# Cutting a sixth product of the second feed-forward stage into a two-level scheme, with two squarings moved to ScalarE

## The chip, the cores and the metric

The kernel runs on one core of a Trainium2 chip. The metric is the device time of one execution in microseconds (us).

## The reference, cut to what matters

An attention block without softmax feeds a feed-forward block whose activation is a scaled square of a relu. All arithmetic is fp32.

```
kv  = einsum('bhsd,bhse->bhde', k, v)            # 8 batches, 8 heads, 576 x 64
out = einsum('bhsd,bhde->bhse', q, kv)
x   = normalised out, transposed and reshaped to (4608, 512)
h   = x @ w_in                                   # 512 x 2048
g   = s * relu(h)**2 + b
y   = g @ w_out                                  # 2048 x 512
```

## The kernel before

The tokens are worked off in nine units of 512. A unit has a first stage (`x @ w_in`) and a second stage (`g @ w_out`). Each stage is a Strassen-Winograd scheme: 2 x 2 blocks, seven products (numbered 1 to 7) instead of eight, and additions on VectorE. From unit 2 on, five of the seven products of the second stage (`TWICE`) are cut up once more in the same way. The weight sums for this second level are formed once in unit 1 and written to DRAM.

```python
TWICE = (1, 2, 6, 7, 4)
ORDER = (1, 2, 6, 7, 5, 3, 4)      # the parts of a two-level product

def parts_of_w(i):                 # unit 1: four sums, seven stores of 256 KB
    ...
    for n, t in enumerate((y11, y21, t2, t3, t1, y22, t4)):
        nc.sync.dma_start(out=w3_dram[i][:, n], in_=t)

def second_level(i, other, to, x_tag="y", y_tag="y"):
    ...
    def go(m, bank, first):        # one part: 4 matmuls of 128x128 into one PSUM bank
        ...
        for f in range(FC // 4):
            matmul(t[bank], a[m][:, f], w[:, f], first and f == 0, f == FC // 4 - 1)
    def keep(name, j, q):          # VectorE reads the bank "x"
        scaled(r[name], t["x"], other(j, cols[q]))
    def m1(): go(1, "x", True);  keep("r1", 0, 0)
    def m2(): go(2, "z", True);  scaled(to(0, cols[0]), t["z"], r["r1"])
    def m6(): go(6, "x", False); keep("r2", 1, 0)
    def m7(): go(7, "y", True)
    def m5(): go(5, "x", False); keep("r4", 1, 1); scaled(to(1, cols[1]), t["y"], r["r4"])
    def m3(): go(3, "x", False); scaled(to(0, cols[1]), t["x"], other(0, cols[1]))
    def m4(): go(4, "y", False); scaled(to(1, cols[0]), t["y"], r["r2"])
```

Parts 1, 6, 5 and 3 add up in one bank "x" (a bank is a piece of PSUM, the memory into which the matmuls add their products), and VectorE reads the bank after each. So part 6 has to wait for the read after part 1, part 5 for that after part 6, part 3 for that after part 5. Something else must stand between them on PE. The scheduling is by hand: each engine gets its instructions in the order of the program. This is the end of a second stage, in program order:

```python
            p7[2]()                # p7[m]: part m of product 7
            pump(1)                # pump: load the next weight tiles into a ring of 7
            p7[6]()
            p7[7]()
            pump(1)
            p7[5]()
            at(3)                  # unit 2 only: an attention product
            def between():
                p7["sums"]((3,)); p4["sums"](); at("sums")
                p7[3](); pump(1); p7[4](); pump(1)
                at(("q", 0)); p4[1](); at("norm")
            x3(0, between)         # product 3, one level, row block 0: 8 matmuls of 128x256
            p4[2](); p4[6](); with_7(0); p4[7](); with_7(1)
            p4[5]()
            at(4)
            at(5)                  # the four sums xs for the next unit's first stage
            x3(1)                  # product 3, row block 1
            pump(4)
            at(("q", 1))
            y4_of(0, 3)            # part 3 of product 4, and stores
            pump(1)
            y4_of(1, 4)
```

## Time and profile before

| | |
|---|---|
| time, median of the first 3 runs | 953.24 us (953.16 to 955.73) |
| time, median of 6 runs, with those taken beside the changed kernel | 954.85 us |
| span of the profiled run | 951.5 us |
| PE busy | 936.3 us |
| one unit's end of second stage, from part 1 of product 6 to the next unit (units 3 to 7) | 25.66 us |

"PE" is the matmul row of TensorE and "PEld" its weight loads. "DVE" is VectorE, "ACT" is ScalarE and "SPq" is the sync engine's queue, which issues the DMAs. In a timeline each line has start, duration, engine, source line, operation, tiles, shape and count, with idle time and its releaser in brackets. All times of TensorE in this text are taken from start to start.

### The profile page before, as it was taken

The page shows a single profiled execution, that of the slowest core. Times are in us where ns is not written, and L with a number is a line of the kernel's source. Part 1 is how long each engine was busy: PE and PEld are TensorE (multiplying, and loading weights), DVE is VectorE, ACT ScalarE, POOL GpSimd, SP SyncE. Part 2 cuts the span into 40 slices and gives each one's busy share as a digit, 9 for nine tenths or more (in the row PEclk, how much of TensorE's full clock was granted, in tenths as well). Part 3 has the DMA queues.
Part 4 walks back from the last instruction along what each step waited for, and adds up shares of the span by engine and source line. Part 5 has one row for each costly group of instructions (what it writes and reads, how often), then busy time and mean ns, then how long its engine had stood idle before and what let it go on. Part 6 is the DMA issues. An engine that isn't in the chain of part 4 may idle for free.

```text
span 951.5 us, 17795 instructions
## 1 busy us (share of the span) xinstructions
PE 936.3 (98%) x7270; PEld 840.1 (88%) x7270; DVE 639.9 (67%) x1167; ACT 191.6 (20%) x366; POOL 6.7 (1%) x18
## 2 busy tenths in 40 slices
PE   7999999999999999999999999999999999999997
PEld 7888888888888998899889988999889988998997
DVE  2789667486567765876478656775678657854684
ACT  2784132101121013200231013101320032001100
POOL 2000000000000000000000000000000000000000
PEclk9999999999999999999999999999999999999999
DMA  9688726578772758165644764375526520653064
GB/s 248 199 317 247 251 79 195 138 221 258 192 190 55 234 155 225 24 193 190 178 110 130 236 185 111 85 248 162 158 51 220 185 92 12 209 180 121 14 222 142
DMA packets 136656, 158.46 MB, mean 167 GB/s; under 512 B 77696, under 2 KB 91776, under 8 KB 136448
## 3 DMA queue, kind: packets, MB, share of 16 engines
q1 hardware_dynamic: 133472, 155.57, 54.7%
q10 hardware_dynamic: 2784, 1.77, 0.8%
q8 instruction: 57, 0.93, 0.4%
q14 instruction: 23, 0.19, 0.1%
q0 software_dynamic: 320, 0.00, 0.0%
HBM read 131.34 MB, written 25.95 MB: 165 GB/s over the span
## 4 chain that ended last, share of the span: by engine, by line
PE 88%; DVE 5%; DMA 3%; ACT 2%; issue 1%; SPq 0%; DVEq 0%; ACTq 0%
PE x_ps L91 41%; PE y_ps L91 25%; PE z_ps L91 9%; PE t_ps L91 8%; PE x_ps L440 3%; PE kv_ps L377 2%; DMA w_raw<-in_moe_w_in_dram 1%; ACT xT L494 1%; DMA kv_sb<-in_k_dram 1%; DMA w_sb<-w 1%; DVE xT L488 1%; DVE a L247 1%; DVE xn L463 1%; DVE a L547 1%; DVE sub L250 0%
## 5 line engine op out<-in xcount | busy, mean ns | idle before, releaser
L592 ACT COPY r<-x_ps 128x512 f32<-128x512 f32 x96 | 56.0, 584 | 405.6 <-PE x_ps L91 383.3
L91 PE MATMUL x_ps<-xs,ws 128*128 128x256 f32 x512 | 122.1, 381 | 0.8 <-ACT r L592 0.4
L91 PE MATMUL y_ps<-xs,wb 128*128 128x256 f32 x512 | 122.6, 382 | 0.3 <-DVE a L247 0.3
L91 PEld LDWEIGHTS x_ps<-xs,ws 128*128 128x128 f32 x512 | 96.4, 190 | 15.9 <-ACT r L592 2.9
L91 PEld LDWEIGHTS y_ps<-xs,wb 128*128 128x128 f32 x512 | 95.5, 190 | 16.0 <-DVE a L247 2.5
L247 DVE TENSOR_TENSOR a<-y_ps,r 128x512 f32<-128x512 f32 x64 | 43.9, 685 | 72.1 <-ACT r L592 60.1
L91 PE MATMUL x_ps<-xT,wa 128*128 128x256 f32 x384 | 89.8, 380 | 0.1
L91 PEld LDWEIGHTS x_ps<-xT,wa 128*128 128x128 f32 x384 | 72.2, 190 | 10.5 <-ACT xT L494 0.5
L91 PE MATMUL x_ps<-w_sb,a 128*128 128x256 f32 (+1 forms) x376 | 79.7, 364 | 0.0
L91 PEld LDWEIGHTS x_ps<-w_sb,a 128*128 128x128 f32 x376 | 66.9, 190 | 8.4 <-issue 0.6
L547 DVE SCALAR_TENSOR_TENSOR a<-a 128x512 f32<-128x512 f32 x96 | 66.4, 691 | 3.1
L91 PE MATMUL y_ps<-w_sb,sub 128*128 128x128 f32 x504 | 62.0, 275 | 0.0
L91 PEld LDWEIGHTS y_ps<-w_sb,sub 128*128 128x128 f32 x504 | 60.2, 192 | 0.7
L91 PE MATMUL x_ps<-xT,ws 128*128 128x256 f32 x256 | 60.5, 379 | 0.0
L91 PE MATMUL z_ps<-xT,wa 128*128 128x256 f32 x256 | 60.5, 379 | 0.0
L91 PE MATMUL x_ps<-w_sb,s 128*128 128x256 f32 x256 | 58.1, 380 | 0.7 <-DMA w_sb<-w 0.7
L91 PE MATMUL t_ps<-w_sb,sub 128*128 128x128 f32 x448 | 54.8, 275 | 0.0
L91 PEld LDWEIGHTS z_ps<-xT,wa 128*128 128x128 f32 x256 | 48.6, 190 | 6.6
L626 DVE TENSOR_TENSOR a<-a 128x512 f32<-128x512 f32 x32 | 22.1, 689 | 47.9 <-ACT a L623 47.9
L91 PEld LDWEIGHTS x_ps<-w_sb,s 128*128 128x128 f32 x256 | 47.4, 190 | 7.2 <-issue 1.1
L91 PE MATMUL y_ps<-w_sb,a 128*128 128x128 f32 (+1 forms) x360 | 53.7, 298 | 0.0
L91 PEld LDWEIGHTS x_ps<-xT,ws 128*128 128x128 f32 x256 | 48.1, 190 | 6.2
(139 smaller groups left out, 1265.9 us busy)
## 6 DMA issues: line engine op xcount, KB each, us to landing
w_sb<-w SPq DMA_DIRECT2D x147, 512.0 KB, 4.9
w_sb<-w SPq DMA_DIRECT2D x35, 256.0 KB, 2.8
w_raw<-in_moe_w_in_dram SPq DMA_DIRECT2D x8, 1024.0 KB, 7.3
w_raw<-in_moe_w_out_dram SPq DMA_DIRECT2D x8, 1024.0 KB, 5.0
w_sb<-in_k_dram SPq DMA_DIRECT2D x48, 144.0 KB, 2.9
w_sb<-in_v_dram SPq DMA_DIRECT2D x48, 144.0 KB, 3.0
out_dram<-o SPq DMA_DIRECT2D x104, 64.0 KB, 2.6
w<-sub SPq DMA_DIRECT2D x20, 256.0 KB, 4.6
```

The lines of the kernel that those rows point to most:

```text
L91: nc.tensor.matmul(o, lhsT=lhsT, rhs=rhs, start=start, stop=stop, skip_group_check=True)
L247: nc.vector.tensor_tensor(out=o, in0=a, in1=b, op=ALU.add)
L377: nc.tensor.matmul(ps[r][l * HB : l * HB + HB, i, :], lhsT=kv[l][rows, 0, j, :], rhs=kv[l][rows, 1, j, :], start=(j == 0), stop=(j == R - 1),)
L440: nc.tensor.matmul(ps[32 * p : 32 * p + 32, w, :], lhsT=st["qT"][:, p, 32 * w : 32 * w + 32], rhs=bd_kv[(b if w < 2 else b1) % 2][:, p, :] ...
L463: nc.vector.tensor_tensor(out=st["xn"].rearrange("p h d -> p (h d)").rearrange("p (c h e) -> p h c e", c=KC, h=H), in0=st["x"].rearrange(" ...
L488: nc.vector.transpose(out=to, in_=st["xn"].rearrange("p h d -> p (h d)").rearrange("p (c x) -> p c x", c=KC))
L494: nc.scalar.activation(to[:, i], to[:, i], AF.Copy, scale=g_col[:, i : i + 1])
L547: nc.vector.scalar_tensor_tensor(t, t, 0.0, t, ALU.max, ALU.mult)
L592: nc.scalar.copy(st[name], src)
L626: nc.vector.tensor_mul(ga["a21", s], ga["a21", s], ga["a21", s])
```

## The change

Product 3 becomes the sixth two-level product. It has 28 matmuls of 128x128 instead of 16 of 128x256. As it no longer adds into product 5's bank, two adds (`with_5`) take over that sum. To make room on VectorE, two squarings of each unit's last step go to ScalarE. And the end of the second stage gets a new order, since the two halves of product 3 no longer exist.

```diff
-    TWICE = (1, 2, 6, 7, 4)
+    TWICE = (1, 2, 6, 7, 4, 3)
 ...
-            relu_sq(t)
+            if u > 1 and s == NS - 1:
+                nc.scalar.activation(t, t, AF.Relu)
+                nc.scalar.square(t, t)
+            else:
+                relu_sq(t)
 ...                                   # x3_square likewise, and it now follows x3 at once
-                lambda: x3(0),
+                seq(lambda: x3(0), lambda: parts_of_w(3)),      # unit 1
 ...
+        def with_5(j):
+            add(right("o1", j), right("o1", j), right("o2", j))
 ...
+            p7["sums"]((3,))
             p7[2](); pump(1); p7[6]()
+            p3["sums"]((5, 6))
             p7[7](); pump(1); p7[5](); at(3)
-            x3(0, between)
+            p3["sums"]((7, 3)); at("sums")
+            p7[3](); pump(1); p7[4](); pump(1)
+            with_5(0); at(("q", 0))
+            p3[1](); p4["sums"]((5, 6)); at("norm")
+            p3[2](); with_5(1); pump(1)
+            p3[6](); p4["sums"]((7, 3)); p3[7](); pump(1)
+            p3[5](); at(4)
+            p4[1]()
+            p3[3](); store("o1", 0, 4 * u); pump(1)
+            p3[4](); store("o1", 1, 4 * u + 1); pump(1)
+            at(5)
             p4[2](); p4[6](); with_7(0); p4[7](); with_7(1); p4[5]()
-            at(4); at(5); x3(1); pump(4)
+            pump(2)
             at(("q", 1)); y4_of(0, 3); pump(1); y4_of(1, 4); pump(1)
```

(Statements of several lines are put on one here.)

More of the change, by code (lines that the diff above doesn't have):

```diff
@@ L625, in x3_square @@
         def x3_square():
-            nc.vector.tensor_mul(ga["a21", s], ga["a21", s], ga["a21", s])
+            if u > 1 and s == NS - 1:
+                nc.scalar.square(ga["a21", s], ga["a21", s])
+            else:
+                nc.vector.tensor_mul(ga["a21", s], ga["a21", s], ga["a21", s])
         def x3_s1():
@@ L874, in x5, with x3 @@
                 store("o2", j, 4 * u + 2 + j, slice(HN, DM))
-        def x3(j, *between):
+        def x3(j):
             product(3, j, st["x", j], False)
-            for fn in between:
-                fn()
-            if u > 1:
-                add(right("o1", j), right("o1", j), b_21)
             scaled(rows("o1", j)[:, HN:], st["x", j], b2 if u == 1 else st["o1", j][:, HN:])
@@ L956, in mm2 @@
         )
+        p3 = second_level(3, lambda j, q: right("o1", j, q), lambda j, q: right("o1", j, q), "x")
         def x5_of(j, *between):
@@ L988, in rest @@
             step["x3"]()
+            step["x3_square"]()
             p2["sums"]()
@@ L991, in rest @@
             pump(1)
-            step["x3_square"]()
             p1[4]()
@@ L1038, in rest @@
             at(3)
-            def between():
-                p7["sums"]((3,))
-                p4["sums"]()
-                at("sums")
-                p7[3]()
-                pump(1)
-                p7[4]()
-                pump(1)
-                at(("q", 0))
-                p4[1]()
-                at("norm")
-            x3(0, between)
+            p3["sums"]((7, 3))
+            at("sums")
+            p7[3]()
+            pump(1)
+            p7[4]()
+            pump(1)
+            with_5(0)
+            at(("q", 0))
+            p3[1]()
+            p4["sums"]((5, 6))
+            at("norm")
+            p3[2]()
+            with_5(1)
+            pump(1)
+            p3[6]()
+            p4["sums"]((7, 3))
+            p3[7]()
+            pump(1)
+            p3[5]()
+            at(4)
+            p4[1]()
+            p3[3]()
+            store("o1", 0, 4 * u)
+            pump(1)
+            p3[4]()
+            store("o1", 1, 4 * u + 1)
+            pump(1)
+            at(5)
             p4[2]()
@@ L1058, in rest @@
             p4[5]()
-            at(4)
-            at(5)
-            x3(1)
-            pump(4)
+            pump(2)
             at(("q", 1))
```

## The prediction

> **What bounds the kernel now.** I read the page first. The busy table says that TensorE is the engine to watch, and the groups say how few and short its waits are.
>
> ```profile
> PE 936.3 (98%) x7270; PEld 840.1 (88%) x7270; DVE 639.9 (67%) x1167; ACT 191.6 (20%) x366; POOL 6.7 (1%) x18
> PEclk9999999999999999999999999999999999999999
> PE 88%; DVE 5%; DMA 3%; ACT 2%; issue 1%; SPq 0%; DVEq 0%; ACTq 0%
> ```
>
> PE is busy for 98% of the span at full clock, and the chain that ended last is PE for 88%. A PE gain should therefore reach the end, and so will any stall put into PE's stream. So I went to PE's timeline in one steady unit (the second stage of one unit in the middle, from 597 to 654 us). Columns: start, duration, engine, line, operation, shape, number of records. One fp32 matmul leaves two records, so a first-level product of one row block (8 matmuls of 128x256) is x16, and one of the seven parts of a second-level product (4 matmuls of 128x128) is x8.
>
> ```profile
> 635.85 2.84 PE L91 MATMUL y_ps<-w_sb,sub 128*128 128x128 f32 x24
> 638.53 3.62 PE L91 MATMUL x_ps<-w_sb,a 128*128 128x256 f32 x16
> 641.98 1.05 PE L91 MATMUL y_ps<-w_sb,sub 128*128 128x128 f32 x8
> 642.88 1.06 PE L91 MATMUL y_ps<-w_sb,a 128*128 128x128 f32 x8
> 643.77 1.06 PE L91 MATMUL t_ps<-w_sb,a 128*128 128x128 f32 x8
> 644.66 1.06 PE L91 MATMUL z_ps<-w_sb,a 128*128 128x128 f32 x8
> 645.55 2.84 PE L91 MATMUL t_ps<-w_sb,sub 128*128 128x128 f32 x24
> 648.24 3.62 PE L91 MATMUL x_ps<-w_sb,a 128*128 128x256 f32 x16
> 651.69 1.05 PE L91 MATMUL t_ps<-w_sb,sub 128*128 128x128 f32 x8
> 652.58 1.06 PE L91 MATMUL t_ps<-w_sb,a 128*128 128x128 f32 x8
> ```
>
> Start to start, the x16 takes 3.45 us and every x8 takes 0.893 us. There is no gap at all from 605 to 653.5 us: the dense second stage is pure PE throughput. The two x16 are product 3, the one that the change cuts up. They do a second job: each stands between part 5 of a two-level product and its part 3, which adds into the same PSUM bank. VectorE has 3.45 us to read the bank before PE needs it. VectorE's timeline there:
>
> ```profile
> 638.73 0.35 DVE L707 SCALAR_TENSOR_TENSOR r<-y_ps,s_col,o 128x128 f32<-128x128 f32 x1 [1.44 <-PE y_ps L91]
> 639.12 0.35 DVE L707 SCALAR_TENSOR_TENSOR or<-y_ps,s_col,r 128x128 f32<-128x128 f32 x1
> 649.09 0.68 DVE L250 TENSOR_TENSOR xs<-xT 128x512 f32<-128x512 f32 x1
> 651.62 0.42 DVE L247 TENSOR_TENSOR o<-o,b 128x256 f32<-128x256 f32 x1
> ```
>
> The first line is the read of part 5 (product 7), 1.1 us after that group's start; the last two bracket the four sums for the next unit, 2.53 us, wholly under the second x16.
>
> **What the Trainium skill says.** "PSUM — Partial Sum Buffer", section "Engine vs sequencer instructions": VectorE and ScalarE queues are strict FIFO, and matmuls start and complete in program order. So a matmul that waits holds all later ones, and a PSUM read behind long sums on VectorE waits for them. The trace agrees: both timelines keep the program's order. "VectorE: DVE Perf Modes", section "The TRN2 errata", gives (N+151)/0.96 ns for an fp32 tensor_tensor, 691 ns at 512 columns; the trace has 0.68 to 0.69 us, but successive ones start 0.60 us apart when independent and 0.72 apart when the second reads the first; I use those spacings. "Perfetto Trace Analysis", section "Tensor Engine Instruction", says that a matmul's end is estimated; so I take PE times from starts.
>
> **The change, part by part.** It concerns units 2 to 8, seven of them; unit 1 prepares the weights.
>
> *PE work.* Removed per unit: 2 x 3.45 = 6.91 us. Added: 7 parts x 0.893 = 6.25 us. Gain 0.66 us per unit, 4.6 us in all, 0.5%. This is all that the change can win, as PE has no wait there to lose.
>
> *VectorE to ScalarE.* Two squarings of about 0.6 us each leave VectorE in each unit's last step. ScalarE is 20% busy, and its copy of 128x512 takes 0.58 us. PE does not wait for VectorE there, so I give it nothing.
>
> *VectorE added.* Four sums of 128x512 (2.5 us), seven reads of 128x128 and two adds of 128x256, less four operations of 128x256: some 3.5 us more per unit, before the squarings. VectorE stays below 85% in these stages; its order matters, not its total.
>
> *New waits on PE.* The order listing shows that in the changed kernel product 7's part 5 is followed at once by its part 3, and likewise product 4's part 5 by part 3, each with a wait on VectorE. What such a wait costs: the read starts 1.09 us after the group's start (part 1 at 643.77, read at 644.86) and takes 0.35. The restart overhead comes from unit 2 of the kernel before, where VectorE was 0.08 us late for such a bank:
>
> ```profile
> 341.92 0.34 DVE L707 SCALAR_TENSOR_TENSOR r<-t_ps,s_col,or 128x128 f32<-128x128 f32 x1
> 342.32 0.97 PEld L91 LDWEIGHTS t_ps<-w_sb,sub 128*128 128x128 f32 x8 [0.15 <-DVE r L707]
> 340.40 3.07 PE L91 MATMUL t_ps<-w_sb,sub 128*128 128x128 f32 x24
> ```
>
> Three groups took 3.07 instead of 2.84, a loss of 0.23, so 0.15 beyond the lateness. A direct chain costs 1.09 + 0.35 - 0.893 + 0.15 = **0.70 us**.
>
> Now one unit by hand, with the first part of product 6 at 627.81 as origin, each group 0.893 later, and the order as listed:
> - Part 5 to part 3 of product 7: +0.70.
> - Part 1 of product 3 then starts at 641.01, is read at 642.10 to 642.37; two dependent sums for product 4 (1.33) end at 643.70; the next read (0.27) and an add (0.38) bring VectorE to 644.35, when it reads part 6; done 644.70. Part 5 wants that bank at 644.58: 0.12 + 0.15 = +0.27.
> - Part 4 of product 3 starts at 647.53 and is read at 648.62. Then VectorE does the four sums for the next unit (2.53), now ahead of product 4's parts 2 and 6 in its queue, and has read part 6 by 652.04. Part 5 of product 4 wants the bank at 651.11: 0.93 + 0.15 = +1.08. Before, these sums lay under the second x16.
> - Part 5 to part 3 of product 4: +0.70.
>
> Sum 2.75, less 0.66: **+2.1 us per unit**, for units 3 to 7: +10.5. Unit 8 makes no sums for a next unit: 0.70 + 0.27 + 0.70 - 0.66 = +1.0. Unit 2 has attention products between product 7's parts 5 and 3 (no first wait) but a row sum, a normalization and a transpose more in VectorE's queue; the same walk gives 1.10, 1.25 and 0.70, less 0.66: +2.4. Together +13.9 us.
>
> *Unit 1.* Four more subtractions (2.5 us) and seven more stores of 256 KB. VectorE is busy 13.8 of 25 us from 225 to 250 us, and PE is fed from tiles loaded long before: nothing.
>
> *Transfers.* A two-level product loads 1.83 MB instead of 1.05. Products 6, 7, 3 and 4 then take 7.3 MB in about 27 us, 272 GB/s; the queue moved 256 to 287 GB/s in the busiest 5 us stretches here, with up to seven tiles ahead. I worked out 3 to 4 us of lead for each tile: hidden.
>
> **The rivals.** (1) *PE work decides*: the waits are covered, the kernel gains 4.6 us, 948.6. For it: PE is gapless and the change is written to thin out VectorE. Against it: a wait straight after the matmul that it depends on cannot be covered by any VectorE. (2) *Mine*: the filler was worth more than the work saved, 967. (3) *Weights come late*: each of the seven units waits a further 1 to 2 us for a tile in products 3 and 4, 972 to 980. For it: demand is close to what the queue has shown, and the kernel before has one DMA wait of 0.7 us. Against: that one is the only one in seven units. (4) *ScalarE's squares or VectorE's relief* remove waits in the units' first parts: at most the 0.3 to 1 us per unit that PE idles in first stages, but those waits stand before the moved operations.
>
> **Range and chances.** 953.2 + 13.9 = **967.1**. The third wait is the least certain, as one VectorE operation earlier or later moves it by 0.5 us per unit, 3.5 in all; if the sums are covered in part, 962. More DMA waiting gives 971. Range 961.5 to 971. Slower by over 2% needs 972.3: 0.06. Faster by over 2% exceeds all that PE work can give: 0.01. Within 2%: 0.93.
>
> **What would show it right or wrong.** PE's timeline after product 7's part 5 and product 4's part 5 should show an idle of 0.4 to 0.5 us in the record (0.7 lost start to start), released by VectorE, in each of units 3 to 8; the one before product 4's part 5 should be absent in unit 8 and about 1.1 in units 3 to 7; x8 groups should keep 0.893. PE's sum of idle should grow by about 15 us and the waits of weight loads on VectorE likewise. If those gaps are missing and the end comes near 948.6, the read is quicker or the order different from what I took. If the gaps name DMA, rival 3 holds. If second stages look the same and first stages differ, rival 4.

## The result, and the profile after

The changed kernel took **971.5 us** (median of 6, 970.51 to 973.76) against 954.85 us for the kernel before. The ratio of fast runs is 1.0181 (95% interval 1.0164 to 1.0198). The profiled run has a span of 968.4 us, 16.9 more.

The page of the changed kernel: the busy shares, then the shares of the chain that ended last.

```profile
PE 938.0 (97%) x7438; PEld 842.9 (87%) x7438; DVE 659.6 (68%) x1220; ACT 204.8 (21%) x387; POOL 6.7 (1%) x18
PE 81%; DVE 10%; DMA 4%; ACT 2%; issue 1%; SPq 1%; DVEq 0%; ACTq 0%
```

VectorE's share of the chain went from 5 to 10% of the span: PE now waits for it. Here is PE's timeline in the unit that the prediction walked through, the same stretch of it:

```profile
644.56 2.84 PE L91 MATMUL y_ps<-w_sb,sub 128*128 128x128 f32 x24
647.85 1.16 PE L91 MATMUL y_ps<-w_sb,sub 128*128 128x128 f32 x8 [0.45 <-DVE r L714]
648.84 1.06 PE L91 MATMUL y_ps<-w_sb,a 128*128 128x128 f32 x8
...
652.42 1.06 PE L91 MATMUL y_ps<-w_sb,sub 128*128 128x128 f32 x8
653.61 1.16 PE L91 MATMUL x_ps<-w_sb,sub 128*128 128x128 f32 x8
654.60 1.06 PE L91 MATMUL t_ps<-w_sb,a 128*128 128x128 f32 x8
...
658.18 1.95 PE L91 MATMUL t_ps<-w_sb,sub 128*128 128x128 f32 x16
660.94 1.16 PE L91 MATMUL t_ps<-w_sb,sub 128*128 128x128 f32 x8 [0.81 <-DVE r L714]
662.54 1.16 PE L91 MATMUL t_ps<-w_sb,sub 128*128 128x128 f32 x8 [0.44 <-DVE r L714]
```

All groups keep their 0.893 us except four. Start to start these lose 0.71 (part 3 of product 7, at 647.85), 0.40 (part 5 of product 3, at 653.61), 1.08 (part 5 of product 4, at 660.94) and 0.71 (part 3 of product 4, at 662.54). A group that starts after a wait also takes 0.99 to 1.00 us to the next one, not 0.89: that is the 0.1 us in each loss that the brackets don't show. The list of PE's waits over the whole changed kernel counts them (us in total, times, longest):

```profile
PE t_ps L91 <- DVE r L714: 8.0, 13, 0.9
PE y_ps L91 <- DVE r L714: 2.7, 6, 0.4
```

The six on y_ps are product 7's part 3 in units 3 to 8; the 13 on t_ps are product 4's part 3 in seven units and its part 5 in six, as unit 8 has no sums for a next unit. PE's idle time (span less busy) went from 15.2 to 30.4 us. VectorE's timeline shows why the wait of product 4's part 5 is the longest:

```profile
652.69 0.41 DVE L247 TENSOR_TENSOR o<-o,o 128x256 f32<-128x256 f32 x1
653.20 0.35 DVE L714 SCALAR_TENSOR_TENSOR r<-x_ps,s_col,o 128x128 f32<-128x128 f32 x1
...
657.75 0.68 DVE L250 TENSOR_TENSOR xs<-xT 128x512 f32<-128x512 f32 x1
...
660.28 0.34 DVE L714 SCALAR_TENSOR_TENSOR o<-z_ps,s_col,r 128x128 f32<-128x128 f32 x1
660.54 0.34 DVE L714 SCALAR_TENSOR_TENSOR r<-t_ps,s_col,or 128x128 f32<-128x128 f32 x1
```

The read at 660.54 is the one that PE's group at 660.94 waits for. It stands behind the four sums for the next unit, from 657.75 to 660.28. Before, the same sums lay under the second half of product 3. The first two lines are an add (`with_5`) and the read behind it, for which PE's group at 653.61 waits.

Milestones of PE in both traces show where the 16.9 us are (time after less time before, each from the starts of PE's groups):

| stretch | before | after | difference |
|---|---|---|---|
| start of the program to unit 2 | 246.86 | 246.58 | -0.28 |
| unit 2, first stage (to part 1 of product 1) | 51.20 | 52.22 | +1.02 |
| unit 2, product 6 to the end | 27.10 | 29.31 | +2.21 |
| unit 3, products 1 to 5 | 24.06 | 25.27 | +1.21 |
| units 3 to 7, product 6 to the end, five times | 25.66 | 27.90 | +11.20 |
| unit 8, product 6 to the last group's start | 24.77 | 25.94 | +1.17 |
| from there to the end of the span | 6.62 | 6.91 | +0.29 |
| all other stretches | | | +0.08 |

The ends of the second stages make 14.6 of the 16.9. The other two larger entries are outside them. In unit 2's first stage PE waits for queries. VectorE's timeline of the changed kernel, then PE's:

```profile
276.62 0.71 DVE L409 STREAM_TRANSPOSE qT<-q_sb 128x512 f32<-128x512 f32 x1 [3.14 <-DMA q_sb<-in_q_dram]
```

```profile
277.48 1.08 PE L440 MATMUL x_ps<-bd_kv,qT 128*32 128x128 f32 x32 [0.94 <-DVE qT L409]
```

VectorE was held for 3.14 us until a DMA had brought queries. In the kernel before it transposed them without a wait (VectorE's timeline, then PE's):

```profile
273.68 0.70 DVE L409 STREAM_TRANSPOSE qT<-q_sb 128x512 f32<-128x512 f32 x1
```

```profile
276.75 1.08 PE L440 MATMUL x_ps<-bd_kv,qT 128*32 128x128 f32 x32
```

The sync engine's queue tells what came in front of these loads. L730 are the stores of weight parts, and L1247 are queries. The changed kernel:

```profile
244.88 1.19 SPq L730 DMA_DIRECT2D w<-w_sb  x2
246.17 1.93 SPq L730 DMA_DIRECT2D w<-sub  x3
248.15 0.66 SPq L730 DMA_DIRECT2D w<-w_sb  x1
248.91 0.69 SPq L730 DMA_DIRECT2D w<-sub  x1
249.64 2.39 SPq L1247 DMA_DIRECT2D q_sb<-in_q_dram  x4
...
271.44 1.83 SPq L1247 DMA_DIRECT2D q_sb<-in_q_dram  x4
```

These seven stores are new. Each issue takes about 0.6 us of the queue, 4.8 us in all up to the next query load. By the program, the transpose at 276.62 needs the queries that L1247 loads. The last four of these loads begin at 271.44, where the kernel before began them at 266.14. Unit 3's entry is the wait for the weight tiles of product 5, which the queue sends late in both kernels:

```profile
PE x_ps L91 <- DMA w_sb<-w: 1.9, 2, 1.3
```

This line of the waits of the changed kernel (us in total, times, longest) read 0.7 us, once, before.

### The profile page after: what moved, and what is told of

Same layout as the page of the kernel before. It is cut to its first block, busy times and chain, and to the rows that moved or that the text cites. A ratio compares the mean times of both kernels' runs of the same rounds, so it can differ in the third digit from the quotient of the medians.

```text
span 968.4 us, 18270 instructions
## 1 busy us (share of the span) xinstructions
PE 938.0 (97%) x7438; PEld 842.9 (87%) x7438; DVE 659.6 (68%) x1220; ACT 204.8 (21%) x387; POOL 6.7 (1%) x18
## 4 chain that ended last, share of the span: by engine, by line
PE 81%; DVE 10%; DMA 4%; ACT 2%; issue 1%; SPq 1%; DVEq 0%; ACTq 0%
PE x_ps L91 36%; PE y_ps L91 25%; PE z_ps L91 8%; PE t_ps L91 7%; PE x_ps L440 3%; DMA w_sb<-w 2%; DVE xs L250 2%; PE kv_ps L377 1%; DVE r L714 1%; DMA w_raw<-in_moe_w_in_dram 1%; DVE sub L250 1%; ACT xT L494 1%; DMA kv_sb<-in_k_dram 1%; DVE xT L488 1%; DVE a L247 1%
## 5 line engine op out<-in xcount | busy, mean ns | idle before, releaser
L91 PE MATMUL y_ps<-w_sb,sub 128*128 128x128 f32 x560 | 70.1, 276 | 2.7 <-DVE r L714 2.7
L91 PEld LDWEIGHTS y_ps<-w_sb,sub 128*128 128x128 f32 x560 | 66.4, 192 | 4.4 <-DVE r L714 3.8
L91 PE MATMUL t_ps<-w_sb,sub 128*128 128x128 f32 x448 | 56.9, 278 | 8.0 <-DVE r L714 8.0
L547 DVE SCALAR_TENSOR_TENSOR a<-a 128x512 f32<-128x512 f32 x89 | 61.5, 691 | 2.8
L91 PEld LDWEIGHTS t_ps<-w_sb,sub 128*128 128x128 f32 x448 | 52.7, 192 | 10.5 <-DVE r L714 10.5
L91 PE MATMUL y_ps<-w_sb,a 128*128 128x128 f32 (+1 forms) x416 | 61.1, 295 | 0.0
L91 PEld LDWEIGHTS y_ps<-w_sb,a 128*128 128x128 f32 x416 | 55.4, 192 | 2.2 <-issue 0.2
L250 DVE TENSOR_TENSOR a<-a,a 128x512 f32<-128x512 f32 x72 | 48.6, 685 | 0.8
```

Of the source, the lines that this page charges most:

```text
L91: nc.tensor.matmul(o, lhsT=lhsT, rhs=rhs, start=start, stop=stop, skip_group_check=True)
L250: nc.vector.tensor_tensor(out=o, in0=a, in1=b, op=ALU.subtract)
L547: nc.vector.scalar_tensor_tensor(t, t, 0.0, t, ALU.max, ALU.mult)
```

## The experiments

My theory: PE decides, and the halves of product 3 were fillers that covered reads of PSUM. Taking them away puts four waits into each second stage, of which one is caused by the place of the next unit's sums. Unit 1's stores add a wait of their own. Rival A: VectorE has too much work in all. Rival B: weights come too late.

**1. The sums for the next unit behind product 4's part 5.**

```diff
-            at(5)
             p4[2](); p4[6](); with_7(0); p4[7](); with_7(1); p4[5]()
             pump(2)
+            at(5)
```

> The changed kernel with one edit: the four sums for the next unit stand after product 4's part 5 instead of ahead of its part 2. My theory (the filler was worth more than the work): the wait before product 4's part 5 falls from 0.8 us of idle to 0 in units 3 to 7 and shrinks in unit 2, the other two waits stay; 1.08 us x 5 + some 1.2 us = 6.6 us less than the changed kernel, so +10.5 us (1.011) against the kernel before. Rival A (VectorE has too much work in all): the same work is still there, so about nothing changes, 1.018. Rival B (late weights): nothing changes, 1.018.

Measured: 965.33 us, 1.012 (1.0103 to 1.0137). In units 4 to 7 the stretch from product 6 to the end took 26.83 us instead of 27.90, 1.07 less. PE's timeline there shows the wait before part 5 gone and that before part 3 left:

```profile
554.04 2.84 PE L91 MATMUL t_ps<-w_sb,sub 128*128 128x128 f32 x24
557.33 1.16 PE L91 MATMUL t_ps<-w_sb,sub 128*128 128x128 f32 x8 [0.44 <-DVE r L714]
```

The first x24 holds parts 6, 7 and 5 without a gap. The same work on VectorE costs 1.07 us less per unit for standing elsewhere, which speaks against rival A.

**2. Product 3's part 4 as a filler between product 4's parts 5 and 3.**

```diff
-            p3[4](); store("o1", 1, 4 * u + 1); pump(1)
             at(5)
             p4[2](); p4[6](); with_7(0); p4[7](); with_7(1); p4[5]()
-            pump(2)
+            p3[4](); store("o1", 1, 4 * u + 1); pump(3)
```

> The changed kernel with one move on PE: product 3's part 4 stands between product 4's part 5 and its part 3. My theory: the wait before part 3 of product 4 (0.44 us of idle, 0.70 start to start) is covered in all seven units, the waits before product 7's part 3 and product 4's part 5 stay: 4.9 us less than the changed kernel, +12.3 us against before (1.013). Rival A (VectorE's load): the wait only moves to the next read, about 1.018. Rival B (late weights): 1.018.

Measured: 966.94 us, 1.0133 (1.0118 to 1.0147). Product 6 to the end took 27.21 us in units 4 to 7, 0.69 less than 27.90. One filler of 0.89 us covers one wait wholly.

**3. Only unit 1's preparations, in the kernel before.** `parts_of_w(3)` is called behind unit 1's first half of product 3, and nobody reads its result.

```diff
-        i: dram.tile([P, 7, FC // 4, P], FP32, name=f"w3_{i}") for i in TWICE
+        i: dram.tile([P, 7, FC // 4, P], FP32, name=f"w3_{i}") for i in TWICE + (3,)
 ...
-                lambda: x3(0),
+                seq(lambda: x3(0), lambda: parts_of_w(3)),
```

> The kernel before, plus only what unit 1 does for the new product: four subtractions and seven stores of 256 KB (nobody reads them). What I had put at nothing. Theory from the trace of the changed kernel: the seven issues take some 4.5 us of the sync engine's queue, the queries for unit 2 arrive later, VectorE waits 3.1 us for them and PE 0.9 us: +0.9 us (1.001), with a PE wait for the transposed queries near 277 us. Rival (VectorE's four subtractions delay something in unit 1): the wait is in unit 1's second stage, before 247 us. Rival (my first reading): 0.

Measured: 955.37 us, 1.0015 (1.0002 to 1.0029). Unit 2's first stage took 53.00 us (51.20 before), with this line in PE's timeline:

```profile
278.03 1.08 PE L440 MATMUL x_ps<-bd_kv,qT 128*32 128x128 f32 x32 [1.73 <-DVE qT L409]
```

The wait is in unit 2's first stage and not in unit 1. The timed difference alone is barely clear of noise; the trace carries the argument. So the stores (or the subtractions with them) cause it, without any of the rest of the change.

**4. The same stores on ScalarE's queue, in the changed kernel.**

```diff
+            queue = nc.scalar if i == 3 else nc.sync
             for n, t in enumerate((y11, y21, t2, t3, t1, y22, t4)):
-                nc.sync.dma_start(out=w3_dram[i][:, n], in_=t)
+                queue.dma_start(out=w3_dram[i][:, n], in_=t)
```

> The changed kernel with the seven new stores of unit 1 issued from ScalarE's queue instead of the sync engine's. If the issue time of the sync queue is what delays unit 2's queries, PE's wait near 277 us goes and the kernel is 0.9 us faster than the changed one: +16.4 us against before (1.017). If it is the bandwidth or the subtractions, nothing changes: 1.018.

Measured: 970.22 us, 1.0169 (1.0155 to 1.0183), 0.0012 less than the changed kernel, as expected in size, though intervals of this width overlap. The trace is clearer: unit 2's first stage took 51.22 us, as in the kernel before, and the list of PE's waits is empty there. VectorE still waited a little for the queries:

```profile
275.07 0.71 DVE L409 STREAM_TRANSPOSE qT<-q_sb 128x512 f32<-128x512 f32 x1 [0.84 <-DMA q_sb<-in_q_dram]
```

The stores move the same bytes and the subtractions are the same, so it is the stores' place in the sync queue that makes PE wait. The other traces agree: unit 2's first stage took 51.20 to 51.23 us in the three of the kernel before, 51.22 to 51.36 in the three with these stores on ScalarE's queue (this run and experiments 8 and 9), and 52.12 to 55.48 in the eight with them on the sync queue. That all of the delay is issue time is not shown: here the last of the awaited query loads still began at 269.50, and the list of waits has the sync queue waiting 2.1 us for a store of this kind to finish (`w<-sub`).

**5. The squarings back on VectorE.** Both branches `u > 1 and s == NS - 1` were taken out.

> The changed kernel with the two squarings of each unit's last step back on VectorE. My reading: PE waits for neither of them, so nothing changes: 1.018 against before. Rival A (VectorE's load sets the time): 14 operations of 0.6 us more on VectorE, in the crowded part: some 8 us more, 1.027.

Measured: 978.46 us, 1.0266 (1.0248 to 1.0283). My expectation was missed, and rival A's number was met. But the trace shows a new wait of PE in product 2, one in each of the seven units:

```profile
628.74 2.94 PE L91 MATMUL y_ps<-w_sb,sub 128*128 128x128 f32 x24 [1.15 <-DVE r L707]
```

VectorE's timeline explains it: the second squaring had to wait for the relu of ScalarE, and the sums and the read that PE needs stood behind it.

```profile
624.68 0.69 DVE L626 TENSOR_TENSOR a<-a 128x512 f32<-128x512 f32 x1 [1.62 <-ACT a L623]
...
628.34 0.34 DVE L707 SCALAR_TENSOR_TENSOR r<-y_ps,s_col,o 128x128 f32<-128x128 f32 x1
```

The change had also moved the squaring to directly behind the relu. On ScalarE that place is harmless; on VectorE it is not. My edit had undone the engine and not the place.

**6. The squarings back on VectorE and at their old place.** The second squaring stands behind the sums of product 2 and part 3 of product 1 again.

> The changed kernel with both squarings back on VectorE, and the second one also back at its old place, behind the sums for product 2 and product 1's part 3. The earlier run had it right behind ScalarE's relu, where VectorE waited 1.6 us for that and PE then 1.15 us for VectorE. If that place was the cause (mine): 1.018, as the changed kernel. If VectorE's load is the cause (rival A): 1.027 again, as the same operations are on VectorE.

Measured: 971.37 us, 1.0177 (1.0161 to 1.0192), against 1.0181 for the changed kernel. Product 6 to the end took 27.90 us in units 4 to 7, as in the changed kernel, with the 14 operations on VectorE. So rival A falls, and in this order ScalarE's part of the change is worth nothing measurable.

**7. The gapless order.** Two fillers and a better order on VectorE: `with_5(1)` early, `with_5(0)` behind part 2 of product 3, the sums for product 4 behind the reads of parts 6 and 5, and the next unit's sums last.

```diff
             p7[5]()
+            with_5(1)
             at(3)
+            p3["g1"](); p3["k1"]()          # matmuls and read of part 1 of product 3
+            p3["sums"]((7,)); at("sums")
             p7[3](); pump(1)
+            p3["sums"]((3,))
             p7[4](); pump(1); at(("q", 0)); at("norm")
-            p3[1](); ...
+            p3[2](); with_5(0); pump(1)
+            p3[6](); p4["sums"]((5, 6)); p3[7](); pump(1)
+            p3[5](); p4["sums"]((7, 3)); at(4)
             p4[1](); p3[3](); store("o1", 0, 4 * u); pump(1)
             p4[2](); p4[6](); with_7(0); p4[7](); with_7(1); p4[5]()
+            p3[4](); store("o1", 1, 4 * u + 1); pump(3)
             at(("q", 1)); y4_of(0, 3); pump(1); y4_of(1, 4); pump(1); at(("q", 2))
+            at(5)
```

> The changed kernel with the same PE work in another order: product 3's part 1 between product 7's part 5 and part 3, product 3's part 4 between product 4's part 5 and part 3, the sums for the next unit last, and VectorE's adds and sums moved so that no read of a bank stands behind two sums. My theory: all four waits go, PE is gapless in the second stages of units 3 to 8 and only the gain of 0.66 us per unit stays: 4.6 us less than before, plus 1 us for unit 1's stores, plus 0 to 1.5 us left in unit 2 and in the late weights of unit 3: -2 to -3.6 us against before (0.996 to 0.998). Rival A (VectorE's load): the same VectorE work as in the changed kernel, so still well above 1.01. Rival B (late weights): with PE quicker the demand rises, DMA waits grow in products 3 and 4 and it stays above 1.0.

Measured: 952.56 us, 0.9986 (0.9971 to 1.0). Product 6 to the end took 25.01 us in units 4 to 7, that is 0.65 less than in the kernel before. That is the pure gain in PE work, and the whole of it. The same VectorE work is done here as in the changed kernel, only in another order, so this run too speaks against rival A. The lines of PE's timeline around product 7's part 5:

```profile
637.50 2.84 PE L91 MATMUL y_ps<-w_sb,sub 128*128 128x128 f32 x24
640.17 1.06 PE L91 MATMUL x_ps<-w_sb,a 128*128 128x128 f32 x8
641.07 1.06 PE L91 MATMUL y_ps<-w_sb,sub 128*128 128x128 f32 x8
```

Part 1 of product 3 now stands between part 5 and part 3, and there is no gap. The total fell short of my -2 to -3.6 us: unit 2's first stage took 53.27 us in this trace (+2.1), and the end of the span came 6.9 us after the last group's end (945.0 to 951.9), against 5.6 before.

**8. The same, with unit 1's stores on ScalarE's queue** (the edit of experiment 4).

> The same as the gapless order, with unit 1's seven new stores issued from ScalarE's queue. My theory: another 0.9 us less, -3 to -4.6 us against before (0.995 to 0.997), and the faster version of all.

Measured: 952.29 us, 0.9984 (0.9968 to 0.9999). Unit 2's first stage fell to 51.35 us and the profiled span to 949.1 us, but the time hardly moved against experiment 7; the expected 0.9 us is not shown by the timed runs, and the whole fell short of my -3 to -4.6 us.

**9. The last store of product 3 on ScalarE's queue, in the last unit only**, on top of experiment 8.

```diff
             p3[4]()
-            store("o1", 1, 4 * u + 1)
+            late_queue = nc.scalar if u == U - 1 else nc.sync
+            store("o1", 1, 4 * u + 1, queues=(late_queue, late_queue))
```

> The gapless order with unit 1's stores on ScalarE's queue, and in the last unit the store of product 3's second row block issued from ScalarE's queue too. In the gapless kernels the time from the last matmul group's end to the end of the span was 6.9 to 7.1 us, against 5.6 before, because this store now stands late in the sync engine's queue. My theory: the tail falls back by some 1.3 us, to about -2.8 us against before (0.997). Rival (the tail is the transfer, not the issue): no change, 0.9984.

Measured: **948.8 us, 0.9951** (0.9938 to 0.9963). The last matmul group ends at 943.0 us and the span at 948.6: the tail is 5.6 us, as before, where the gapless kernels had 6.9 and 7.1. In the trace 3.9 us come from units 3 to 8 (six times 0.65). The time fell further than I expected (-2.8 us against before; by medians it is -5.3). From experiment 8 to this one the ratio fell by 0.0033, some 3.1 us, of which the shorter tail explains 1.5; the rest is not explained. This is the fastest version, and faster than both kernels.

**10. Half of unit 3's query loads later, in the changed kernel.** 32 loads go from the first stage to the end of the second.

> The changed kernel with 32 small query loads of unit 3 moved from the first stage to the end of its second stage, where unit 2 has them. In the changed kernel the sync engine's queue is busy with 64 of these until 10.7 us into the second stage, and the tiles of product 5 come late: PE waits 1.9 us for them against 0.7 before. If the queue's issue time is the cause, both waits go: 1.9 us less than the changed kernel, +15.4 us (1.016). If it is bandwidth alone, the waits stay: 1.018.

Measured: 981.05 us, 1.0291 (1.0273 to 1.0308): a miss for the whole, and a hit for the place. Unit 3's products 1 to 5 took 22.86 us with no wait for weights, 2.4 less than 25.27. So these loads make product 5's tiles late there: in the changed kernel they hold the sync queue for 39.03 us in one run of 64 issues (376.50 to 415.53), and the first of these tiles is issued behind them at 416.10, 3 us before PE could use it. Whether it is their issue time or their bytes is not separated, as the run moves both. But the queries that unit 4 has to transpose came too late, and PE waited 10.17 us at once. PE's timeline:

```profile
497.96 3.66 PE L91 MATMUL x_ps<-xT,ws 128*128 128x256 f32 x8 [10.17 <-ACT r L592]
```

VectorE waited 14.9 us for query transfers in unit 4's first stage (the list of waits has two, the longer of 12.9), and the stage took 64.4 us instead of 52.4. In this trace unit 2's first stage, which the edit does not touch, took 55.48 us too, 3.3 more than in the changed kernel, so the total is not the edit's alone.

**11 and 12. The kernel before, twice more**, for traces.

> The kernel before, unchanged, for another trace. Is unit 3's wait for the tiles of product 5 larger because of the change? From the start of product 1 to the start of product 6 in unit 3 the kernel before took 24.06 us in its one trace, the changed kernel 25.27, other kernels with two-level product 3 24.3 to 25.6, and 22.87 without any wait. If the change causes it: again close to 24.1. If it varies from run to run in either kernel: anything up to 25.6.

> The same once more: close to 24.1 us for that stretch if the change causes the longer wait, up to 25.6 if it varies from run to run.

Measured: 954.21 and 954.3 us (one run each). Unit 3's products 1 to 5 took 23.88 and 24.29 us, after 24.06 in the first trace. The kernels with a two-level product 3 (without experiment 5, which has a wait of its own there, and experiment 10) had 24.29, 24.33, 24.46, 24.92, 25.04, 25.07, 25.27 and 25.58 us, one trace each; the kernel with the stores alone had 25.04. The two ranges touch, and no trace of either kernel is at the 22.87 us without waits. The stretch varies from run to run, and how much of unit 3's +1.21 us belongs to the change stays open.

## Why the prediction was right or wrong

The direction, the mechanism and the class were right: slower, and within 2%. The number was not: 971.5 us lies half a microsecond above the range and 4.4 above the forecast. Of that, 1.6 us is the base. The rest is in the traces, which differ by 16.9 us where I had 13.9: 1.0 of these 3.0 us is unit 2's first stage, 1.2 unit 3's product 5, 0.7 the second stages, and 0.1 what is left. Step by step:

- *PE work, -0.66 us per unit*: right. Experiment 7 isolates it at -0.65.
- *Direct chains, +0.70 each*: right, measured 0.71 and 0.71. One filler takes one away (0.69, experiment 2).
- *Part 5 of product 4 behind the next unit's sums, +1.08*: right, measured 1.08, and 1.07 by taking it away (experiment 1).
- *Part 5 of product 3, +0.27*: low, measured 0.40. I had let the read follow the add 0.38 us later, the spacing of independent operations. The read uses what the add wrote, and the trace has 0.51 (652.69 to 653.20); two such pairs in the kernel before have 0.45 and 0.52. Together the walk gave 2.1 us per unit where the trace has 2.24. Over units 3 to 8 that is some 0.9 us low, and unit 2 was 0.2 high (2.4 against 2.21): its three losses came out at 1.24, 1.15 and 0.71 where I had 1.10, 1.25 and 0.70, but I had not taken off the 0.23 us that the kernel before loses there, although I had used that very loss for the restart overhead.
- *"Unit 1 ... nothing"*: **the step that failed**. I looked at VectorE's load and at the weight tiles, and not at the queue that issues the stores. Standing in that queue, the stores delayed unit 2's queries, VectorE waited 3.14 us for them and PE 0.94. It cost 1.02 us in the first trace, 0.9 to 2.1 in six of the seven other traces with those stores on the sync queue, and 4.3 in that of experiment 10; experiment 3 shows it alone (53.00 us instead of 51.20), and experiment 4 takes PE's wait away.
- *Transfers hidden*: only partly right. Products 3 and 4, where I had looked for it, have no DMA wait. Product 5 in unit 3 has, +1.21 in the first pair of traces; how much of it is the change's is open (experiments 11 and 12). The supply was larger than I gave it: the view of time windows has 332 GB/s for the kernel before from 637 to 642 us, where I had 287 for the busiest stretch.
- *The base*: I added to 953.24, the median of three runs. With three more runs of it the median was 954.85. 13.9 on top of that would have been 968.8, 2.7 below the result; that the base was low is bad luck of three runs and no fault of the reasoning.

Of the rivals, PE work alone (1) fell: its waits are not covered, and only a new order, with the stores of experiments 8 and 9 on another queue, comes to 948.8, near its 948.6. Late weights (3) did not appear where it put them. ScalarE's squarings (4) are worth nothing measurable in this order (experiment 6).

## What to carry to other kernels

A piece of work on the bounding engine can do a second job as a filler between two steps that depend on each other through another engine; before cutting it up, list which waits it covers, and keep a piece of the new work for each. On an engine that works in program order, where an operation stood counted for more here than how busy the engine was: the same four sums cost 0 or 1.08 us per unit, and the same two squarings 0 or 1.4 us per unit. The queue that issues DMAs is such an engine too, and seven added stores belong into its timeline before they are called free.

## What the Trainium skill lacked or had wrong

- "DMA: Bandwidth & Descriptors", section "Issuing engines are not separate DMA queues", says that the time to initiate a DMA "is usually small relative to the DMA itself". That holds here for one DMA: about 0.6 us per issue on the sync engine, where such stores took 3.4 to 3.7 us (medians) from issue to landing. What the section leaves out is that issues add up in a queue: 4.8 us for seven stores, and 39.03 us for one run of 64 query loads. The same stores from ScalarE's queue took PE's wait away.
- "Perfetto Trace Analysis", section "Tensor Engine Instruction", gives no cost of holding up a stream of matmuls. Here a group of eight records that had waited took 0.99 to 1.00 us to the next instead of 0.89, so 0.1 us on top of the wait itself.
- "VectorE: DVE Perf Modes", section "The TRN2 errata", has the duration of an fp32 tensor_tensor right (691 ns at 512 columns; 0.68 to 0.69 us here), but not the spacing of two of which the second reads what the first wrote: 0.72 us from start to start here, against 0.60 for independent ones. My low term for part 5 of product 3 was of this kind (0.51 instead of 0.38 us behind a 128x256 add).
- No page gives a measured spacing of fp32 matmuls in this pattern (how many passes they take and how far apart bf16 matmuls start stand on separate pages). Here it was 0.216 us per record of 128x256 and 0.112 per record of 128x128, two records to a matmul, at a granted clock of 0.999.
